# Raw slots and fixed places for the first layer's made w2 sets

## The chip, the cores and the metric

The kernel runs on one core of a Trainium2 chip. The metric is the time of one execution on the device in microseconds; the kernel before takes 1995.99 us, the median of three runs (1995.85 to 1996.73). The engines named below are PE (TensorE, matmuls), DVE (VectorE), ACT (ScalarE), POOL (GpSimd) and SP (SyncE, which here issues every DMA).

## The reference

Three layers follow one another: windowed attention, a gated layer with one expert, and a layer of eight experts whose outputs are weighted by a doubly normalised router. All data are float32.

```python
scores = scale * q @ k.T                      # 4 batches, 8 heads, 576 positions, 64 wide
mask   = (rel >= 0) & (rel < 64)              # each position sees itself and 63 before it
attn   = softmax(where(mask, scores, -1e9)) @ v
x  = attn.transpose(0, 2, 1, 3).reshape(2304, 512)

g  = x @ w_gate                               # 512 x 1536          "first layer"
x  = (g * sigmoid(g) * (x @ w_val)) @ w_out   # 1536 x 512

P  = exp(x @ r_gate - max)                    # router, 8 experts
for _ in range(8):
    P /= P.sum(1); P /= P.sum(0); P *= 2304 / 8
out = sum(P[:, e] * (relu(x @ w1[e]) @ w2[e]) for e in range(8))   # "second layer"
```

## The kernel before

**Precision.** A float32 product is made of three products of a faster type: each operand is split into a high part (a cast on ACT) and a low part (a subtraction on DVE). So every weight that is loaded is split before PE can use it.

**First layer.** The 2304 tokens are 18 tiles of 128 in five blocks (4, 4, 4, 4 and 2 tiles). A block runs 12 steps `f`, 60 steps in all; a step uses three weights: gate and value (`emit_gv`, 12 matmuls each, L788) and output (`emit_o`, 12 matmuls, L806, one step later). Each step's three places in the source are "positions", 180 in all. In block 0 the weights are read as they are, converted and stored in a DRAM buffer `saved`; in blocks 1 to 4 (from step 12) they are loaded from `saved`, 256 KB each, and split by `split_1` (ACT L605, DVE L606) two steps ahead of their use.

**Attention beside it.** Each step of the first layer carries pieces of the attention of the next block's tiles, a tile every nine positions: transposes of q and k (L297), scores (PE L320), their reduction (DVE L332, eight a tile), exponentials (ACT L409), normalisation (DVE L417, L418, L423), transposes of the result (PE L440) and the product with v (L457). After a block, the router's logits are computed from its output (L826, DVE L841, PE L853, DVE L856), and ACT copies the output from PSUM (L816) for a store to `x2d` (L818).

**The made w2 sets.** The second layer multiplies with seven combinations (a Strassen scheme) of the quarters of a pair of w2 blocks. For the experts 1 to 5 the combinations are made during the first layer and stored in the DRAM buffer `w2p`: 20 sets of two raw blocks (2 x 256 KB) that become seven pieces of 256 KB, high and low parts together. `split_w2q` (L718) makes one set in three parts: `w2_first` (ACT L678 and twice L675, DVE L687, L700, L701), `w2_second` (ACT L675, DVE twice L684) and `w2_third` (ACT twice L675, DVE L715, L716 and three times L684), and ends with one store of all seven pieces (L731, 1792 KB). It works in one of two staging places in turn (`o_stw`).

**The ring of raw slots.** All raw weights (from `saved`, the sets' two blocks, x for the second layer, the first w1 and w2) are loaded by `load_one` (L560) in the order in which they are used, each into the next slot of a ring: six slots (`o_raw`) up to step 12, then eight (`o_raw` and two of the second layer's accumulators, `o_more`) to the end of the first layer, then six again (`place_raws`). A load is issued when the use that held its slot is done; a set holds its two slots until the end of `split_w2q`.

**Order.** The source emits the pieces in the order of the positions, and a scheduler sets each engine's order from that and from what it expects to be ready; it may move an instruction ahead of others or behind them. Only where the source asks for it (`add_manual_dep` at the end) an instruction is kept behind a given one. SP's queue is in order too: a DMA that waits for its data or its slot holds up those behind it. The first layer's sets stand one after a step in two of three steps, from step 12 on, and are not tied.

Of the kernel before, what the change touches and what calls it, by code (L numbers as in the profile page):

```python
# [17 lines left out]
def attention_moe_moe2(  # L18
# [78 lines left out]
    o_ones = take("F", 128)  # L97
    o_mask = take("F", 3 * WK)
    o_logit = take("F", NTILE * NE)
    o_prob = take("F", NTILE * NE)  # L100
    o_rows = take("F", NTILE)
    o_cols = take("F", NE)
    o_part = take("F", NE)
    o_gmax = take("F", 2)
    o_stat = take("F", NSC * 3 * H)
    o_lgs = takes("F", 128, 6)
    o_wgp = take("F", KD * 32)
    NRAW = 6
# [12 lines left out]
    o_more = o_acc[4:6]  # L121
# [6 lines left out]
    o_kraw = takes("bF", 512, 3)  # L128
    o_xc = take("bR", 2 * 7 * 2 * HT)
# [18 lines left out]
    o_stw = [o_w2[0], o_w2[4]]  # L148

# [57 lines left out]
    def emit_consts():  # L207
# [19 lines left out]
        nc.gpsimd.memset(ones, 1.0)  # L227
# [292 lines left out]
    raw_at = []  # L520
    raw_prev = []
    raw_done = set()
    raw_held = set()

    def place_raws(ready):
        ring = o_raw + o_more
        last = {}
        for n in range(len(raw_keys)):
            if n < 2 * NCONV:
                o = o_raw[n % NRAW]  # L530
            elif n < ready:
                o = ring[(n - 2 * NCONV) % len(ring)]
            else:
                o = next(raw_at[i] for i in range(n - len(ring), n) if raw_at[i] in o_raw and last[raw_at[i]] == i)
            raw_at.append(o)
            raw_prev.append(last.get(o))
            last[o] = n
# [7 lines left out]
    def load_one():  # L545
        n = w_load[0]
        if n >= raw_stop[0] or n >= 2 * NCONV and raw_prev[n] is not None and raw_prev[n] not in raw_done:
            return False
        w_load[0] += 1
        key, i = raw_keys[n]  # L550
        src = sources(key)[i]
        if wide(key):
            dst = sl(o_wide[n % NWIDE], 1024).bitcast(I32)
        elif key[0] == "x":
            dst = sl(raw_at[n], HT)
        else:
            dst = sl(raw_at[n], 512)
# [50 lines left out]
    def raw_slots(key):  # L608
# [4 lines left out]
        return [raw_at[n + i] for i in range(cnt)]  # L613
# [109 lines left out]
    def split_w2q(key):  # L723
        _, e, g, j = key
        r = [sl(o, 512) for o in raw_slots(key)]
        st = o_stw[(e * NF2 // 2 + j) % 2]
        o = lambda m: st + 512 * MSEQ.index(m)
        w2_first(r, o)
        w2_second(r, o)
        w2_third(r, o)  # L730
        nc.sync.dma_start(out=kept(e, j), in_=sl(st, 7 * 512).rearrange("p (m w) -> p m w", m=7))  # L731
        load_w()
        load_w()
# [41 lines left out]
    def do_split(key):  # L775
        {"1": split_1, "w1": split_w1, "w2": split_w2, "w2q": split_w2q, "x": split_x}[key[0]](key)
# [82 lines left out]
    def emit_gmax1():  # L859
        nc.vector.tensor_reduce(sl(o_gmax, 1), logit, AX.X, ALU.max)  # L860
# [606 lines left out]
    made = [("w2q", e, 0, j) for e in range(1, NE - 2) for j in range(NF2 // 2)]  # L1467
    seq = [(b, f) for b in range(NB) for f in range(NF1)]
    prev = None
    for s, (b, f) in enumerate(seq):  # L1470
        for kind in range(3):
# [12 lines left out]
            att_at(3 * s + kind)  # L1484
        if s == 1:
# [7 lines left out]
    assert not made  # L1493
# [89 lines left out]
    raw_first = []  # L1583
    for e in ev:
# [9 lines left out]
        if e[0] == "w1n" and key is not None and not raw_first:  # L1594
            raw_first.append(len(raw_keys))
        if key is not None:
            raw_keys.extend((key, i) for i in range(len(sources(key))))

    place_raws(raw_first[0])
# [22 lines left out]
    def banks(x):  # L1622
# [46 lines left out]
        "w2h": emit_w2h,  # L1669
        "w2r": emit_w2r,  # L1670
# [14 lines left out]
    for e in ev:  # L1685
# [56 lines left out]
```

## Time and profile before

| | |
|---|---|
| time, median of three runs | 1995.99 us |
| the profiled execution | 1994.68 us |
| its span | 1992.9 us |
| busy PE, DVE, ACT, POOL | 1965.0, 1509.4, 1233.9, 41.2 us |
| DMA queue of SP | 81.2% of 16 engines' time, 527 MB |
| first layer's steps in the span | about 44 to 571 us |
| second layer | from 571 us to the end |

Times within the profile count from the span's start. A bracket `[2.85 <-DVE area_bF L423]` behind an instruction says that its engine was idle for 2.85 us before it and what ended that idle time. `area_F`, `area_aR` and so on are large tiles that the kernel cuts up itself: `area_F` holds the raw slots, `area_aR` the staging places of the sets. DRAM inputs appear without digits, so `in_moe_w_dram` stands for w1 and w2 as well.

### The profile page before, as it was taken

Reading aid. Unit: us, or ns where it says so; the run is one execution under the profiler, and the core shown is the slowest. Engines: PE = TensorE matmul, PEld = TensorE weight load, DVE = VectorE, ACT = ScalarE, POOL = GpSimd, SP = SyncE. Lnnn points to the kernel's source line nnn. Section 1 sums busy time; section 2 is a strip of 40 time slices with the busy share of each in tenths; the row PEclk is TensorE's granted clock in tenths of the full one; section 3 lists DMA queues with packets and bytes.
Section 4 is the critical chain, followed back from the end, with each engine's and each line's share of the span. In section 5 each row is a group of like instructions: output and inputs, shape, how many; then the busy total and the mean of one; then the engine's idle time right before and its main releaser. Section 6 shows DMA issues by size and latency. Waiting matters only on the chain.

```text
span 1992.9 us, 33648 instructions
## 1 busy us (share of the span) xinstructions
PE 1965.0 (99%) x11815; PEld 1855.9 (93%) x11815; DVE 1509.4 (76%) x3298; ACT 1233.9 (62%) x2795; POOL 41.2 (2%) x77
## 2 busy tenths in 40 slices
PE   8999999999999999999999999999999999999998
PEld 6887877778998999999999999999999999999998
DVE  7987777877677999989987777868777566666566
ACT  7766676766552677777764566657565455555555
POOL 3100000000000000000000000000000000000000
PEclk9999999999999999999999999999999999999999
DMA  9988889777764869979888889989877877777775
GB/s 243 280 271 253 247 230 290 240 242 222 230 225 166 302 212 296 369 244 342 264 287 268 262 301 325 333 301 333 289 248 267 279 260 261 261 260 246 268 240 170
DMA packets 303002, 529.36 MB, mean 266 GB/s; under 512 B 74976, under 2 KB 159728, under 8 KB 302320
## 3 DMA queue, kind: packets, MB, share of 16 engines
q1 hardware_dynamic: 302832, 527.21, 81.2%
q8 instruction: 93, 1.52, 0.3%
q14 instruction: 77, 0.63, 0.1%
HBM read 390.74 MB, written 136.39 MB: 265 GB/s over the span
## 4 chain that ended last, share of the span: by engine, by line
PE 91%; DVE 3%; DMA 3%; ACT 2%; issue 0%; SPq 0%; POOL 0%; DVEq 0%; ACTq 0%
PE ps L1138 34%; PE ps L1271 34%; PE ps L788 12%; PE ps L806 6%; DMA area_F<-in_moe_w_dram 2%; PE ps L965 2%; PE ps L919 2%; PE ps L457 1%; PE ps L440 1%; ACT area_bF L409 0%; PE ps L297 0%; PE ps L320 0%; PE ps L1301 0%; DVE area_R L606 0%; DVE area_bF L423 0%
## 5 line engine op out<-in xcount | busy, mean ns | idle before, releaser
L1138 PE MATMUL ps<-area_bR,area_R 128*128 128x384 f32 x3864 | 771.5, 335 | 0.0
L1271 PE MATMUL ps<-area_R 128*128 128x384 f32 x3864 | 770.6, 334 | 0.0
L1138 PEld LDWEIGHTS ps<-area_bR,area_R 128*128 128x128 f32 x3864 | 678.0, 188 | 1.6 <-ACT area_F L1306 0.3
L1271 PEld LDWEIGHTS ps<-area_R 128*128 128x128 f32 x3864 | 678.5, 188 | 0.0
L1196 DVE TENSOR_TENSOR area_R<-area_aG,area_R 128x384 fp32r<-128x384 f32 x637 | 350.9, 554 | 238.5 <-ACT area_R L1192 232.9
L1192 ACT CAST area_R<-area_aG 128x384 fp32r<-128x384 f32 x637 | 327.0, 514 | 306.3 <-PE ps L1271 256.0
L788 PE MATMUL ps<-area_R 128*128 128x512 f32 (+1 forms) x1068 | 234.8, 374 | 3.3 <-ACT area_F L793 3.3
L788 PEld LDWEIGHTS ps<-area_R 128*128 128x128 f32 x1068 | 188.2, 190 | 41.9 <-ACT area_F L793 3.9
L1261 ACT COPY area_SF<-ps 128x384 f32<-128x384 f32 x320 | 152.5, 478 | 86.8 <-PE ps L1271 84.3
L1170 DVE TENSOR_TENSOR area_aG<-area_aG 128x384 f32<-128x384 f32 x364 | 197.1, 552 | 4.3
L675 ACT CAST area_R<-area_F 128x256 fp32r<-128x256 f32 x284 | 115.4, 407 | 59.8 <-PE ps L1138 42.7
L1239 ACT COPY ps<-area_SF 128x384 f32<-128x384 f32 x280 | 135.4, 485 | 6.8 <-DVE area_SF L1265 2.6
L1148 DVE TENSOR_TENSOR area_F<-area_F,ps 128x384 f32<-128x384 f32 x184 | 101.1, 549 | 38.7 <-PE ps L1138 38.2
L684 DVE TENSOR_TENSOR area_R<-area_F,area_R 128x256 fp32r<-128x256 f32 x284 | 117.7, 416 | 12.3 <-ACT area_R L675 11.6
L806 PE MATMUL ps<-area_SR,area_R 128*128 128x512 f32 (+1 forms) x540 | 122.7, 376 | 0.2 <-ACT area_SR L797 0.2
L1150 ACT COPY area_F<-ps 128x384 f32<-128x384 f32 x184 | 88.4, 480 | 39.8 <-PE ps L1138 39.1
L1160 DVE SCALAR_TENSOR_TENSOR area_aG<-ps,area_F 128x384 f32<-128x384 f32 x182 | 100.6, 553 | 15.2 <-PE ps L1138 15.2
L806 PEld LDWEIGHTS ps<-area_SR,area_R 128*128 128x128 f32 x540 | 93.5, 190 | 18.4 <-issue 1.2
L1160 DVE SCALAR_TENSOR_TENSOR area_aG<-area_F 128x384 f32<-128x384 f32 x182 | 100.3, 551 | 1.3
L606 DVE TENSOR_TENSOR area_R<-area_F,area_R 128x512 fp32r<-128x512 f32 x108 | 74.3, 695 | 32.5 <-ACT area_R L605 20.6
L605 ACT CAST area_R<-area_F 128x512 fp32r<-128x512 f32 x108 | 65.9, 620 | 51.3 <-PE ps L788 17.6
L788 PE MATMUL ps<-area_R,area_SR 128*128 128x512 f32 (+1 forms) x372 | 81.5, 368 | 1.4 <-ACT area_R L470 1.4
(171 smaller groups left out, 1623.3 us busy)
## 6 DMA issues: line engine op xcount, KB each, us to landing
area_R<-w2p SPq DMA_DIRECT2D x322, 512.0 KB, 5.1
area_R<-w1p SPq DMA_DIRECT2D x182, 512.0 KB, 4.4
w1p<-area_R SPq DMA_DIRECT2D x98, 512.0 KB, 5.9
area_F<-in_moe_w_dram SPq DMA_DIRECT2D x160, 256.0 KB, 5.7
area_F<-saved SPq DMA_DIRECT2D x144, 256.0 KB, 4.7
w2p<-area_aR SPq DMA_DIRECT2D x20, 1792.0 KB, 9.2
w2p<-area_F SPq DMA_DIRECT2D x12, 1536.0 KB, 8.6
saved<-area_F SPq DMA_DIRECT2D x18, 512.0 KB, 6.9
```

The costliest lines, as they stand in the source:

```text
L675: nc.scalar.copy(as_r(sl(o, 256)), src)
L684: nc.vector.tensor_tensor(out=as_r(v[:, 256:512]), in0=src, in1=v[:, 0:256], op=ALU.subtract)
L788: nc.tensor.matmul(ps, lhsT=w3[:, kk, :], rhs=x3[:, kk, :], start=(i == 0), stop=(i == 3 * KD - 1))
L806: nc.tensor.matmul(PS[m][:, 0:n], lhsT=sl(o + 512 * wp + m * 128, 128, True), rhs=sl(oh + 512 * xp, n, True), start=(f == 0 and i == 0), s ...
L1138: nc.tensor.matmul(ps, lhsT=sl(o + wp * 256 + kk * 128, 128, True), rhs=sl(o_xc + xp * 14 * HT + (B_OF[m] * 2 + kk) * HT, HT, True), start ...
L1160: nc.vector.scalar_tensor_tensor(out=sl(o_c[at], HT), in0=c, scalar=0.0, in1=sl(o_p[k % 2][q_ % 2], HT), op0=ALU.max, op1=ALU.mult)
L1170: sub = lambda o, a, b: nc.vector.tensor_tensor(out=o, in0=a, in1=b, op=ALU.subtract)
L1192: nc.scalar.copy(sl(o, HT, True), src)
L1196: nc.vector.tensor_tensor(out=sl(o + HT, HT, True), in0=src, in1=sl(o, HT), op=ALU.subtract)
L1239: nc.scalar.copy(l2_bank(n, dt), macc(MSEQ[i], dt))
L1261: nc.scalar.copy(macc(m, dt), l2_bank(7 * k + i, dt))
L1271: nc.tensor.matmul(l2_bank(7 * k + i, dt), lhsT=sl(o + wp * 256 + dt * 128, 128, True), rhs=sl(jit_of[w] + hp * HT, HT, True), start=(j == ...
```

## The change

The first layer's sets leave the ring. They get raw slots of their own (two of the accumulators for the even sets; `o_spare` in another tile and `o_late` for the odd ones, where `o_late` also holds the router's small tiles later), and the ring has six slots throughout. Each set's three parts are emitted at fixed positions, two sets in nine positions; the loads of set n + 2 are emitted behind the third part of set n. The store is cut into five DMAs (two pieces after the first part, twice one after the second, one and two after the third), each emitted one part after its data. All instructions of a part on DVE, ACT and SP are kept behind the newest instruction that the source had emitted on that engine. The ones for the router's column sums are set later, in `emit_gmax1`.

```diff
-    o_ones = take("F", 128)
+    o_late = take("F", 512)
+    o_prob, o_rows, o_ones = o_late, o_late + NTILE * NE, o_late + HT
...
-    o_more = o_acc[4:6]
...
+    o_qraw2 = [o_acc[4:6], [o_spare, o_late]]
+    QSETS = [(e, j) for e in range(1, NE - 2) for j in range(NF2 // 2)]
...
-        if n >= raw_stop[0] or n >= 2 * NCONV and raw_prev[n] is not None and raw_prev[n] not in raw_done:
+        if n >= raw_stop[0] or n >= 2 * NCONV and n - NRAW not in raw_done:
...
-    def split_w2q(key):
...
-        nc.sync.dma_start(out=kept(e, j), in_=sl(st, 7 * 512).rearrange("p (m w) -> p m w", m=7))
-        load_w()
-        load_w()
+    def q_set(n):
+        e, j = QSETS[n]
+        r = [sl(o, 512) for o in o_qraw2[n % 2]]
+        return e, j, r, o_stw[n % 2], lambda m: o_stw[n % 2] + 512 * MSEQ.index(m)
+
+    def emit_qload(n):
+        if n < len(QSETS):
+            e, j, r, st, o = q_set(n)
+            for dst, src in zip(r, w2_sources(e, j)):
+                nc.sync.dma_start(out=dst, in_=src)
+
+    def emit_qstore(n, part):
+        if 0 <= n < len(QSETS):
+            e, j, r, st, o = q_set(n)
+            at = lambda i, k, d=1: sl(st + 512 * i, 512 * (k * d)).rearrange("p (k m w) -> p k m w", m=d, w=512)[:, :, 0]
+            v = kept(e, j)
+            for i, k in ((5, 2),) if part == 0 else ((0, 1), (2, 1)) if part == 1 else ((1, 1), (3, 2)):
+                nc.sync.dma_start(out=v[:, i:i + k, :], in_=at(i, k))
+
+    def emit_q(n, part):
+        e, j, r, st, o = q_set(n)
+        if part == 0:
+            emit_qstore(n - 1, 2)
+            w2_first(r, o)
+        elif part == 1:
+            emit_qstore(n, 0)
+            w2_second(r, o)
+        else:
+            emit_qstore(n, 1)
+            w2_third(r, o)
+            emit_qload(n + 2)
...
     def emit_gmax1():
+        nc.gpsimd.memset(ones, 1.0)
...
-    made = [("w2q", e, 0, j) for e in range(1, NE - 2) for j in range(NF2 // 2)]
+    sets_at = {}
+    for n in range(len(QSETS)):
+        for part, i in enumerate(((2, 3, 5), (6, 8, 9))[n % 2]):
+            sets_at.setdefault(3 * NF1 + 9 * (n // 2) + i, []).append(("q", n, part))
+    sets_at.setdefault(3 * NF1 - 3, []).append(("qload", 0))
+    sets_at.setdefault(3 * NF1, []).append(("qload", 1))
...
+            for e in sets_at.pop(3 * s + kind, []):
+                add(*e)
...
-        if s >= NF1 and s % 3 < 2 and made and (b, f) < (NB - 2, 9):
-            add("split", made.pop(0))
...
-        if e[0] == "w2h":
+        if e[0] in ("w2h", "q"):
+            engines = [mybir.EngineType.DVE, mybir.EngineType.Activation]
+            if e[0] == "q":
+                engines.append(mybir.EngineType.SP)
             for ins in added[begin:]:
-                if ins.engine in (mybir.EngineType.DVE, mybir.EngineType.Activation):
+                if ins.engine in engines:
                     tc.add_manual_dep(
```

What this makes of the queues, at three places. In the kernel after, lines are numbered a little differently: L544 is the ring's load (L560 before), L716 a set's load, L724 a set's store, L589 and L590 the split (L605, L606), L659, L662, L668 and L671 the pieces' casts and subtractions (L675, L678, L684, L687), L797, L799, L801, L802 are L793, L795, L797, L798, and L822 is the store to `x2d`.

SP's queue in the kernel before, up to the third block's end (`saved` and `in_moe_w_dram` are loads into the ring, the latter of the sets' blocks; `w2p` is the set's store):

```order
L731 DMA w2p<-area_aR 896x1x512
L560 DMA area_F<-in_moe_w_dram 128x512
L560 DMA area_F<-saved 128x512 x5
L560 DMA area_F<-in_moe_w_dram 128x512
L560 DMA area_F<-saved 128x512
L731 DMA w2p<-area_aR 896x1x512
L560 DMA area_F<-in_moe_w_dram 128x512
L560 DMA area_F<-saved 128x512
L560 DMA area_F<-in_moe_w_dram 128x512
L253 DMA area_F<-in_v_dram 128x8x64
L560 DMA area_F<-saved 128x512 x3
L818 DMA x2d<-area_F 128x4x512
```

The same stretch of SP's queue in the kernel after:

```order
L253 DMA area_F<-in_v_dram 128x8x64
L724 DMA w2p<-area_aR 128x512
L544 DMA area_F<-saved 128x512
L724 DMA w2p<-area_aR 128x512
L716 DMA area_bF<-in_moe_w_dram 128x512
L716 DMA area_F<-in_moe_w_dram 128x512
L544 DMA area_F<-saved 128x512
L724 DMA w2p<-area_aR 128x512
L724 DMA w2p<-area_aR 128x2x512
L544 DMA area_F<-saved 128x512
L724 DMA w2p<-area_aR 128x2x512
L822 DMA x2d<-area_F 128x4x512
```

Before, a set's two loads stand apart, behind the store of the set before it and among the ring's other loads; after, they stand together, the stores are small and spread, and only `saved` goes through the ring.

ACT's queue ahead of the exponentials of the tile at that block's end, before (`area_aR` is the set's staging place):

```order
L793 ACTIVATE area_F<-ps_72 128x512
L678 CAST area_aR<-area_F 128x2x256
L605 CAST area_R<-area_F 128x512
L675 CAST area_aR<-area_F 128x256 x2
L797 CAST area_SR<-area_F 128x512
L675 CAST area_aR<-area_F 128x256 x2
L409 ACT_TABLE_LOAD
L409 ACTIVATE area_bF,area_F<-area_bF,area_F 128x128 x8
```

ACT's queue at the same place, after:

```order
L662 CAST area_aR<-area_F 128x2x256
L797 ACTIVATE area_F<-ps_72 128x512
L659 CAST area_aR<-area_F 128x256
L589 CAST area_R<-area_F 128x512
L659 CAST area_aR<-area_F 128x256 x2
L801 CAST area_SR<-area_F 128x512
L409 ACT_TABLE_LOAD
L409 ACTIVATE area_bF,area_F<-area_bF,area_F 128x128 x8
```

The set's first cast moved ahead of L793, and the two casts of its third part, which stood between L797 and the exponentials, moved behind them.

DVE's queue from the last score reduction of that tile to its normalisation, before:

```order
L332 ISA area_bF,area_F<-ps_75,area_F 128x128
L332 ISA area_F 128x1
L684 TENSOR_TENSOR area_aR<-area_F,area_aR 128x256
L716 TENSOR_TENSOR area_F<-area_F 128x256
L684 TENSOR_TENSOR area_aR<-area_F,area_aR 128x256
L606 TENSOR_TENSOR area_R<-area_F,area_R 128x512
L684 TENSOR_TENSOR area_aR<-area_F,area_aR 128x256
L417 TENSOR_SCALAR area_F<-area_F 128x8
L418 RECIPROCAL area_F<-area_F 128x8
L423 TENSOR_TENSOR area_bF<-area_bF,area_F 128x1024
```

DVE's queue there after, with what stands ahead of the first reduction in the second piece:

```order
L332 ISA area_bF,area_F<-ps_75,area_F 128x128
L332 ISA area_F 128x1
L668 TENSOR_TENSOR area_aR<-area_F,area_aR 128x256
L417 TENSOR_SCALAR area_F<-area_F 128x8
L418 RECIPROCAL area_F<-area_F 128x8
L423 TENSOR_TENSOR area_bF<-area_bF,area_F 128x1024
```

```order
L799 TENSOR_TENSOR area_F<-area_F,ps_73 128x512
L590 TENSOR_TENSOR area_R<-area_F,area_R 128x512
L668 TENSOR_TENSOR area_aR<-area_F,area_aR 128x256
L802 TENSOR_TENSOR area_SR<-area_F,area_SR 128x512
L332 ISA area_bF,area_F<-ps_74,area_F 128x128
```

One piece of a set is left between the reductions and the normalisation; the third part's other instructions moved behind L423. PE's order is the same but for L853, which stands one or two matmuls earlier after three of the blocks.

## Rows read from the trace of the kernel before

**Rows 1.** Busy time in four stretches: us, each engine busy (instructions), clock, DMA share, GB/s.

```profile
44.00:160.00 116.00, 115.11 (x736) 93.55 (x737) 103.65 (x182) 80.41 (x149) 12.99 (x15) 0.97 0.91 272
160.00:505.00 345.00, 331.42 (x2035) 267.48 (x2034) 252.46 (x616) 226.38 (x517) 15.86 (x24) 1.00 0.80 246
505.00:571.00 66.00, 65.77 (x497) 62.39 (x497) 45.19 (x95) 39.96 (x84) 0.00 (x0) 1.00 0.74 240
...
660.00:1992.90 1332.90, 1327.01 (x7675) 1324.75 (x7673) 999.96 (x2155) 822.86 (x1871) 0.00 (x0) 1.00 0.82 277
```

**Rows 2.** Waits of PE from 160 to 505: us in total, times, longest.

```profile
PE ps L440 <- DVE area_bF L423: 8.4, 5, 3.5
PE ps L853 <- DVE area_F L332: 3.1, 2, 1.7
PE ps L297 <- ACT area_F L793: 1.1, 2, 0.6
PE ps L320 <- DVE area_F L841: 0.9, 1, 0.9
```

**Rows 3.** Busy time as in Rows 1, the two slices around 416.

```profile
400.00:420.00 20.00, 17.15 (x103) 13.75 (x102) 12.21 (x37) 13.05 (x35) 1.36 (x2) 0.98 0.59 183
420.00:440.00 20.00, 20.00 (x120) 15.76 (x119) 14.39 (x29) 11.54 (x23) 0.00 (x0) 0.94 0.98 323
```

**Rows 4.** PE in order of time, 402 to 422: start, duration, instructions.

```profile
406.76 1.10 PE L320 MATMUL ps<-area_F,area_bF 64*64 64x128 f32 x32
...
413.41 2.88 PE L788 MATMUL ps<-area_R,area_SR 128*128 128x512 f32 x12
419.14 1.94 PE L440 MATMUL ps<-area_F,area_bF 128*128 128x128 f32 x8 [2.85 <-DVE area_bF L423]
```

**Rows 5.** DVE in order of time, 402 to 420.

```profile
410.25 0.68 DVE L795 TENSOR_TENSOR area_F<-area_F,ps 128x512 f32<-128x512 f32 x1
...
412.27 0.68 DVE L798 TENSOR_TENSOR area_SR<-area_F,area_SR 128x512 fp32r<-128x512 f32 x1
412.87 0.28 DVE L332 CUSTOM_DVE_ANT_0 area_bF<-ps,area_F 128x128 f32<-128x128 f32 x1
```

**Rows 6.** ACT in order of time, 402 to 420.

```profile
408.52 0.62 ACT L678 CAST area_aR<-area_F 128x512 fp32r<-128x512 f32 x1 [3.71 <-DMA area_F<-in_moe_w_dram]
```

**Rows 7.** SP's issues in order of time, 395 to 420.

```profile
398.12 0.52 SPq L731 DMA_DIRECT2D w2p<-area_aR  x1
...
402.95 1.18 SPq L560 DMA_DIRECT2D area_F<-in_moe_w_dram  x1
```

**Rows 8.** Waits of ACT from 160 to 505.

```profile
ACT area_aR L678 <- DMA area_F<-in_moe_w_dram: 18.7, 11, 4.2
ACT area_aR L675 <- DMA area_F<-in_moe_w_dram: 14.8, 14, 3.8
...
ACT area_R L605 <- DMA area_F<-saved: 9.0, 5, 2.5
```

**Rows 9.** The chain of waits, 258 to 325: start, us, what.

```profile
305.79 10.20 DMA area_F<-in_moe_w_dram
```

**Rows 10.** DMA issues from 160 to 505: times, KB each, median us to landing.

```profile
w2p<-area_aR SPq DMA_DIRECT2D x19, 1792.0 KB, 9.2
area_F<-saved SPq DMA_DIRECT2D x106, 256.0 KB, 5.2
area_F<-in_moe_w_dram SPq DMA_DIRECT2D x39, 256.0 KB, 6.2
```

**Rows 11.** Waits of ACT from 505 to 571.

```profile
ACT area_R L605 <- DMA area_F<-saved: 3.5, 2, 3.1
```

**Rows 12.** DMA issues from 505 to 571.

```profile
area_F<-saved SPq DMA_DIRECT2D x25, 256.0 KB, 3.8
area_F<-in_moe_w_dram SPq DMA_DIRECT2D x16, 256.0 KB, 3.2
```

**Rows 13.** PE's groups by line and shape, 160 to 505.

```profile
L440 PE MATMUL ps<-area_F,area_bF 128*128 128x128 f32 x80 | 11.4, 289 | 8.5 <-DVE area_bF L423 8.4
```

More of the change, by code (lines that the diff above doesn't have):

```diff
@@ L96, in attention_moe_moe2 @@
     o_ident = take("F", 128)
-    o_ones = take("F", 128)
+    o_late = take("F", 512)
+    o_prob, o_rows, o_ones = o_late, o_late + NTILE * NE, o_late + HT
+    o_cols = o_rows + NTILE
+    o_part = o_cols + NE
+    o_gmax = o_part + NE
     o_mask = take("F", 3 * WK)
     o_logit = take("F", NTILE * NE)
[L100 to L104, printed above, removed]
     o_stat = take("F", NSC * 3 * H)
+    o_wgp = take("F", KD * 32 + 16)
     o_lgs = takes("F", 128, 6)
-    o_wgp = take("F", KD * 32)
     NRAW = 6
@@ L128, in attention_moe_moe2 @@
     o_kraw = takes("bF", 512, 3)
+    o_spare = take("bF", 512)
     o_xc = take("bR", 2 * 7 * 2 * HT)
@@ L226, in emit_consts @@
         nc.gpsimd.tensor_copy(sl(o_maskr + 2 * WK, WK, True), sl(o_mask + 2 * WK, WK))
-        nc.gpsimd.memset(ones, 1.0)
         nc.gpsimd.memset(sl(o_wgp, KD * 32), 0.0)
@@ L518, in attention_moe_moe2 @@
     w_next = [0]
-    raw_at = []
-    raw_prev = []
     raw_done = set()
     raw_held = set()
[L525 to L537, printed above, removed]
     def load_w():
@@ L554, in load_one @@
         elif key[0] == "x":
-            dst = sl(raw_at[n], HT)
+            dst = sl(o_raw[n % NRAW], HT)
         else:
-            dst = sl(raw_at[n], 512)
+            dst = sl(o_raw[n % NRAW], 512)
         if len(src.shape) == 3:
@@ L612, in raw_slots @@
         w_next[0] += cnt
-        return [raw_at[n + i] for i in range(cnt)]
+        return [o_raw[(n + i) % NRAW] for i in range(cnt)]
     def wr_slot(kind, b, f):
@@ L775, in do_split @@
     def do_split(key):
-        {"1": split_1, "w1": split_w1, "w2": split_w2, "w2q": split_w2q, "x": split_x}[key[0]](key)
+        {"1": split_1, "w1": split_w1, "w2": split_w2, "x": split_x}[key[0]](key)
     def emit_gv(b, f, kind):
@@ L1466, in attention_moe_moe2 @@
     }
-    made = [("w2q", e, 0, j) for e in range(1, NE - 2) for j in range(NF2 // 2)]
+    sets_at = {}
[4 more added lines that the diff above has]
+    sets_at.setdefault(3 * NF1, []).append(("qload", 1))
+    last_set = max(sets_at) + 1
+    sets_at[last_set] = [("qstore", len(QSETS) - 1, 2)]
     seq = [(b, f) for b in range(NB) for f in range(NF1)]
@@ L1488, in attention_moe_moe2 @@
             add("split", key)
-        if s >= NF1 and s % 3 < 2 and made and (b, f) < (NB - 2, 9):
-            add("split", made.pop(0))
         prev = (b, f)
-    assert not made
+    assert not sets_at
     late = [("w1", 0, 0, 2), ("w2", 0, 0, 6), ("w1", 0, 0, 3), ("w2", 0, 0, 7)]
@@ L1581, in attention_moe_moe2 @@
     assert not hooks and not att and not early and not late, (hooks, att, early, late)
-    raw_first = []
     for e in ev:
@@ L1593, in attention_moe_moe2 @@
             key = ("w2q", e[1], 0, e[2])
-        if e[0] == "w1n" and key is not None and not raw_first:
-            raw_first.append(len(raw_keys))
         if key is not None:
             raw_keys.extend((key, i) for i in range(len(sources(key))))
-    place_raws(raw_first[0])
     marked = []
@@ L1669, in attention_moe_moe2 @@
         "w2h": emit_w2h,
+        "q": emit_q,
+        "qload": emit_qload,
+        "qstore": emit_qstore,
         "w2r": emit_w2r,
```

7 lines of the change are left out of this document (removed).

## Prediction, made before the result

> **What bounds the kernel now.** I read the busy time by stage first, because an average over the whole span (TensorE 99% busy) hides where the rest is. A stage's idle time is its length less TensorE's busy time: 0.9 us from 44 to 160, 13.6 us from 160 to 505, 0.2 us from 505 to 571, and 5.9 us in the second layer, where it lies in the last output tiles [rows 1]. The diff works from step 11 of the first layer's 60, shortly before 160, to that layer's end, so at most some 14 us of waiting are within its reach. The list of TensorE's waits in that stage adds up to the same: 8.4 + 3.1 + 1.1 + 0.9 = 13.5 us, the greatest for the attention's normalised scores (L440 after L423) [rows 2]. To this comes the clock: 0.98 and 0.94 of 2.4 GHz are granted in the two slices around the wait at 416. That is some 3.2 us at the lower level, 1.2 GHz, and costs 20 x 0.02 + 20 x 0.06 = 1.6 us [rows 3].
>
> Then I followed one wait to its cause. The score matmuls L320 end at 407.86, TensorE's other work at 413.41 + 2.88 = 416.29, and L440 starts at 419.14, after 2.85 us of nothing [rows 4]. Its chain is VectorE's score reductions L332, ScalarE's exponentials L409, VectorE's L423. L332 began only at 412.87, five microseconds after its scores were there [rows 5], because ScalarE had sat 3.71 us until 408.52 on L678, the first cast of a made w2 set, waiting for that set's load [rows 6], and VectorE's share of the set stood ahead of L332 in its queue. That load was issued at 402.95, right behind the set before's 1792 KB store of 398.12 [rows 7]: a load is issued when its ring slot comes free, and the sets, which hold two slots until their last part, free them late. So it is in all the stage: ScalarE waits 18.7 + 14.8 us for w2 loads, in 25 waits [rows 8], and a load that lands in 6.2 us at the median takes up to 10.2 us there [rows 9, 10].
>
> The span is 1992.9 us and the profiled run 1994.68, so 1.8 us lie around the span and stay. The median of three runs, 1995.99, is 1.31 us above the profiled run; I take the saving off the median.
>
> **The change part by part.**
>
> *Loads of the sets.* The same 40 loads of 256 KB go into four slots of their own, each issued when set n-2 has finished its third part. Sets alternate over nine positions of the schedule, so between that point and the set's first part lie six positions or more. The 106 saved weights, three a step, take 345 us, so a position (a third of a step) is 345 / 106 = 3.25 us, and six are 19.5 us, against 6.2 us to land at the median and 10.2 at worst [rows 1, 9, 10]. The 33.5 us of ScalarE's waits go. What TensorE gets back of it: of L440's 8.4 us the two great waits, 3.5 and the 2.85 at 416, whole, and of the remaining 2.05 us in three small waits half, 1.0; the 3.1 us of L853 and the 0.9 of L320, where VectorE was late with the set's parts; the 1.1 of L297, where L793 stood behind a waiting cast [rows 2, 4]. Sum 6.35 + 1.0 + 3.1 + 0.9 + 1.1 = 12.4 us. Bounds: 0 and 13.5.
>
> *Clock.* The drop came directly after the 2.85 us wait. Without that wait I take it as gone: 1.6 us; bounds 0 and 1.6 [rows 3].
>
> *Parts at fixed places.* The instructions are the same in number and kind (six on ScalarE and ten on VectorE a set), so their busy time is no term. What they can do is stand ahead of the score chain. L332 to L440 took 419.14 - 412.87 = 6.27 us, so L332 has to start by 416.29 - 6.27 = 410.02 for no wait. In the new order VectorE has L795, one split, one 256-wide piece and L798 between the matmuls' end (406.76) and L332: four of at most the 0.68 us of L795 and L798, 2.7 us, so L332 starts near 409.5, half a microsecond in time [rows 4, 5]. Between L332 and L417 there is one piece, where there were four and a split. So no wait, but a small margin. That is why I leave half of the three small waits standing. Nothing on PE but L853 moves: it stands one or two matmuls earlier after three block ends, losing at most four matmuls of cover, 4 x 2.88/12 = 1.0 us; at least 0. I take 0.3.
>
> *Stores.* One store of 1792 KB becomes three of 256 and two of 512 KB, each issued one part after its data, so SP doesn't stand on them. Nothing waits for them but the staging slots, written again two sets later. Cost nothing, hidden by those nine positions, 29 us; the cover goes if the queue fills (a rival below).
>
> *Ring of six instead of eight.* Between 160 and 505 the ring now holds saved weights alone: six slots of 3.25 us are 19.5 us ahead, less 5.2 us to land [rows 10], no cost. In the last block it is dearer: 25 saved and 16 other loads in 66 us, 1.6 us each, so two slots less are 3.2 us less lead [rows 1, 12]. ScalarE already waits there 3.5 us in two waits, 3.1 the longest, at no cost to TensorE [rows 11, 1]. Bounds: 0, and 2 x 3.2 = 6.4 us if both grow by all of it and pass straight through. Since 3.1 us passed without a trace, I stay near the low end: 1.0.
>
> *The rest.* Moving the router's small tiles and the memset of ones on POOL costs nothing: POOL does nothing from 505 to 571, and the ones are wanted well after the router's maximum, where the memset now stands [rows 1].
>
> Sum: 12.4 + 1.6 - 0.3 - 1.0 = 12.7 us. The profiled run would be 1982.0, the median 1995.99 - 12.7 = **1983.3**. The least and the most: all waits and the clock gone at no cost, 1995.99 - 13.6 - 1.6 = 1980.8; the large terms half as large and the costs at their bounds, 6.2 + 0.8 - 1.0 - 6.4, next to nothing.
>
> **The rivals.**
>
> *Only part comes back.* The great waits go, but the margin of half a microsecond is eaten by sets that now run every period at the same point: all ten tiles of the stage (80 matmuls of L440 at eight each [rows 13]) lose 0.6 us, and the clock drops at another place. Then 12.7 - 6.0 - 0.8 = 6 us, 1990. For it: the margin. Against: five of ten tiles have no wait today though sets run beside them.
>
> *The small stores choke the queue.* The DMA engines are 0.80 busy in the stage; 0.20 x 345 us / 20 sets = 3.45 us more engine time a set would fill them, and the loads would be late however early they are issued [rows 1]. A 256 KB transfer lands in 5.2 us, the 1792 KB store in 9.2, so five small ones one after another are up to 5 x 5.2 - 9.2 = 16.8 us dearer, and at least nothing, as the bytes are the same [rows 10]. If they choke, the waits stay: 1996, no change. Against: the next stage moves the second layer's data at a higher rate, 277 GB/s against 246 [rows 1]. The Trainium skill states this rule in "DMA: Bandwidth & Descriptors", section "Measured (HBM→SBUF, 128 partitions, SWDGE, issued from GpSimd)": batch transfers to 1 MiB or more for three quarters of the peak rate. By it the old store was rightly large and the new ones are not, and the sum would be 0 instead of 12.7; the trace shows transfers overlapping, which one-at-a-time figures leave out, so I give it a small chance.
>
> *SP holds the ring (slower).* The sets' stores and loads are now tied into SP's order, 140 of them, and each waits there for ScalarE or VectorE; behind them stand the saved loads, with six slots. From the point where SP stands longer than 19.5 - 5.2 = 14.3 us on one of them, a split waits, and with it the exponentials behind it on ScalarE. If each of the ten tiles then loses what 416 lost, 2.85 us, that is 28.5 us against 14 removed: 1995.99 + 14.5 = 2010. For it: ScalarE already waits 9.0 us for saved loads here [rows 8]. Against: a part comes at most a few positions after the store's place.
>
> **How the numbers follow.** This kernel's runs tell 0.2%, 4 us, from no change: faster is under 1992.0, slower over 2000.0. Forecast 0.68, within 1980 to 1988; a part only 0.15, 1988 to 1992; choked, or balanced by new waits, 0.09 within 4 us of now, half of it just above 1992; slower 0.06; faster than 1980 0.02. Faster: 0.68 + 0.15 + 0.02 = 0.85. The range 1980 to 1992 holds 0.83.
>
> **What would show it.** Right: between about 160 and 505 TensorE's idle time falls from 13.6 to 3 us or less, ScalarE's waits for w2 loads (33.5 us) to under 5, and the granted clock is full in 400 to 440; the stage ends some 12 us earlier and everything behind keeps its length. The last block's ScalarE waits for saved weights grow from 3.5 us with TensorE's idle time under 1.5 us. Wrong: L440 still waits for L423 on most tiles (the order in the queues, not the loads, was the cause); the median time of w2 loads over 10 us (the queue); SP waiting over 14 us ahead of saved loads; or over 3 us of TensorE idle in the last block (the ring).

## The result, and the profile after

The kernel after takes 1978.48 us, the median of four runs (1977.31 to 1978.88); the kernel before took 1996.36 us in the same rounds (1995.85 to 1999.62). The ratio is 0.9907, 95% interval 0.9894 to 0.9920: 17.9 us less, where 12.7 less were forecast. The profiled execution took 1977.31 us, with a span of 1975.5, 17.3 less than before. In the kernel after, lines lie four or five further on: L792 is L788 of before, L810 is L806, L857 is L853; the splits are L589, the sets' casts L659 and L662.

Busy time by stage in the kernel after, with stages cut where its layer ends; columns as in [rows 1]:

```profile
44.00:160.00 116.00, 115.63 (x751) 94.24 (x752) 101.10 (x176) 81.47 (x156) 13.64 (x15) 1.00 0.90 279
160.00:490.00 330.00, 330.00 (x2043) 268.12 (x2042) 253.45 (x622) 226.91 (x512) 16.88 (x25) 1.00 0.80 254
490.00:553.00 63.00, 61.09 (x474) 58.06 (x473) 42.88 (x90) 37.21 (x79) 0.00 (x0) 1.00 0.73 229
```

The 13.6 us of idle TensorE between 160 and 505 are gone to the last digit, and the clock is full there. Behind the first layer everything keeps its length: 1422.7 us to the span's end, where it was 1422.2. The last block lost 1.9 us where it lost 0.2. All waits of TensorE that the kernel after has between 160 and 560 (us in total, times, longest) lie in that block:

```profile
PE ps L792 <- ACT area_F L797: 1.0, 2, 0.6
PE ps L792 <- DVE area_F L799: 0.8, 1, 0.8
```

ScalarE's waits from 160 to 490 that answer to [rows 8]; no wait for a set's load is left, where there were 33.5 us:

```profile
ACT area_R L589 <- PE ps L792: 21.8, 23, 1.5
...
ACT area_R L589 <- DMA area_F<-saved: 6.3, 4, 3.1
```

The DMA issues of the same stretch answer to [rows 10] (a quarter of the sets' loads go to another tile):

```profile
area_F<-saved SPq DMA_DIRECT2D x105, 256.0 KB, 3.4
w2p<-area_aR SPq DMA_DIRECT2D x39, 512.0 KB, 5.5
w2p<-area_aR SPq DMA_DIRECT2D x60, 256.0 KB, 3.7
area_F<-in_moe_w_dram SPq DMA_DIRECT2D x29, 256.0 KB, 3.7
```

I compared where each of the 60 steps starts in the two traces. The difference grows by 3.4 us before step 2, by 16.8 from there to step 41, where the sets end, shrinks by 1.8 in the last block, and by 1.0 more from its last step to the end of the span: 3.4 + 16.8 - 1.8 - 1.0 = 17.4.

### The profile page after: what moved, and what is told of

It is laid out like the page before. It is cut to its first block, busy times and chain, and to the rows that moved or that the text cites. A ratio compares the mean times of both kernels' runs of the same rounds, so it can differ in the third digit from the quotient of the medians.

```text
span 1975.5 us, 33856 instructions
## 1 busy us (share of the span) xinstructions
PE 1959.5 (99%) x11815; PEld 1853.0 (94%) x11815; DVE 1507.1 (76%) x3298; ACT 1234.5 (62%) x2795; POOL 46.0 (2%) x77
## 4 chain that ended last, share of the span: by engine, by line
PE 94%; DMA 2%; ACT 2%; DVE 1%; SPq 1%; issue 0%; POOL 0%; DVEq 0%; ACTq 0%
PE ps L1143 34%; PE ps L1276 34%; PE ps L792 12%; PE ps L810 7%; PE ps L970 2%; PE ps L924 2%; DMA area_F<-in_moe_w_dram 1%; PE ps L457 1%; DMA area_F<-saved 1%; PE ps L440 1%; PE ps L320 1%; PE ps L297 0%; ACT area_bF L402 0%; PE ps L1306 0%; ACT area_aF L559 0%
## 5 line engine op out<-in xcount | busy, mean ns | idle before, releaser
L792 PE MATMUL ps<-area_R 128*128 128x512 f32 (+1 forms) x1068 | 232.3, 371 | 4.6 <-ACT area_F L797 3.8
L792 PEld LDWEIGHTS ps<-area_R 128*128 128x128 f32 x1068 | 186.2, 188 | 43.1 <-ACT area_F L797 4.7
L659 ACT CAST area_R<-area_F 128x256 fp32r<-128x256 f32 x284 | 115.5, 407 | 60.4 <-PE ps L1143 40.8
L668 DVE TENSOR_TENSOR area_R<-area_F,area_R 128x256 fp32r<-128x256 f32 x284 | 118.1, 417 | 9.5 <-ACT area_R L659 8.9
L810 PE MATMUL ps<-area_SR,area_R 128*128 128x512 f32 (+1 forms) x540 | 121.8, 374 | 0.0
L810 PEld LDWEIGHTS ps<-area_SR,area_R 128*128 128x128 f32 x540 | 92.9, 189 | 17.8 <-issue 1.2
L590 DVE TENSOR_TENSOR area_R<-area_F,area_R 128x512 fp32r<-128x512 f32 x108 | 74.5, 696 | 39.1 <-ACT area_R L589 24.7
L589 ACT CAST area_R<-area_F 128x512 fp32r<-128x512 f32 x108 | 66.0, 621 | 53.6 <-PE ps L792 28.4
L792 PE MATMUL ps<-area_R,area_SR 128*128 128x512 f32 (+1 forms) x372 | 81.3, 368 | 1.9 <-ACT area_R L470 1.3
```

The lines of the kernel that those rows point to most:

```text
L659: nc.scalar.copy(as_r(sl(o, 256)), src)
L668: nc.vector.tensor_tensor(out=as_r(v[:, 256:512]), in0=src, in1=v[:, 0:256], op=ALU.subtract)
L792: nc.tensor.matmul(ps, lhsT=w3[:, kk, :], rhs=x3[:, kk, :], start=(i == 0), stop=(i == 3 * KD - 1))
L810: nc.tensor.matmul(PS[m][:, 0:n], lhsT=sl(o + 512 * wp + m * 128, 128, True), rhs=sl(oh + 512 * xp, n, True), start=(f == 0 and i == 0), s ...
```

## The experiments

Theory: the sets' loads were issued too late, and their slots and early issue cured it ("loads", later "lead"). Rivals: the fixed places, or the order that the scheduler made ("places", "order"); the small stores, because loads land sooner behind them ("stores", in the last four runs "landing"). Idle is TensorE's sum of waits from 160 to 495 (to 505 in the last four), ScalarE's waits are those for set loads with the longest of one; both are read from each run's list of waits. Each ratio is to the kernel before in the same rounds, where its median was 1993.2 to 1996.4 us; that is why times and ratios don't follow each other exactly.

| run | us | ratio, 95% | idle | ScalarE, longest |
|---|---|---|---|---|
| before | 1996.4 | 1 | 13.5 | 33.5, 4.2 |
| after | 1978.5 | 0.9907 (0.9894 to 0.9920) | 0 | 0 |
| after_again | 1976.7 | 0.9914 (0.9895 to 0.9933) | 0 | 0 |
| loads_late | 1997.6 | 1.0012 (0.9999 to 1.0025) | 14.4 | 41.8, 4.7 |
| loads_mid | 1978.7 | 0.9919 (0.9902 to 0.9936) | 0 | 0.8, 0.8 |
| untied | 1987.5 | 0.9960 (0.9946 to 0.9974) | 6.0 | 20.8, 4.1 |
| tie_sp | 1989.1 | 0.9978 (0.9966 to 0.9990) | 8.1 | 32.2, 3.4 |
| tie_compute | 1977.9 | 0.9916 (0.9903 to 0.9930) | 0 | 0 |
| one_store | 1977.5 | 0.9908 (0.9890 to 0.9926) | 0 | 0 |
| loads_only | 1978.4 | 0.9924 (0.9910 to 0.9937) | 0.2 | 11.4, 2.1 |
| ring8 | 1977.3 | 0.9910 (0.9892 to 0.9927) | 0 | 0 |
| ring8_swap | 1976.9 | 0.9915 (0.9901 to 0.9928) | 0 | 0 |
| before_small | 1978.1 | 0.9918 (0.9901 to 0.9935) | 0 | 17.1, 1.8 |
| small_same_all | 1980.6 | 0.9932 (0.9914 to 0.9950) | 0.4 | 11.6, 1.5 |
| small_same_order | 1977.7 | 0.9915 (0.9901 to 0.9930) | 0 | 7.3, 2.1 |
| swap_same_order | 1989.6 | 0.9972 (0.9961 to 0.9983) | 6.6 | 19.7, 4.3 |
| large_other_order | 2025.4 | 1.0146 (1.0127 to 1.0165) | 28.5 | 60.8, 7.6 |

**How early the loads are issued.** loads_late and loads_mid change nothing in the kernel after but the position at which a set's loads are emitted (one or three ahead of its first part instead of six); SP's tie on them stays:

```diff
-            emit_qload(n + 2)
...
+    for n in range(len(QSETS)):
+        sets_at.setdefault(3 * NF1 + 9 * (n // 2) + (1, 5)[n % 2], []).append(("qload", n))   # mid: (-1, 3)
```

> The kernel after, but each set's two loads are issued one position (some 3.2 us) ahead of its first part instead of six; slots of their own, fixed places and small stores stay. Theory 'loads': a load lands in about 6 us at the median, so ScalarE waits some 3 us for most of the 20 sets, about 40 us or more in all between 160 and 500, and TensorE is idle there again for 8 to 20 us; 1988 to 2000 us. Rival 'places': the fixed places keep the score chain ahead of a late set; ScalarE waits, TensorE is idle for under 3 us, 1978 to 1982 us.

> The kernel after, but each set's loads are issued three positions (some 9.8 us) ahead of its first part, where the kernel after has six (no wait, 1978 us) and the late version one (42 us of ScalarE waits, 1997.6 us). Theory 'lead': what counts is whether the lead covers the landing; the loads land in 3 to 6 us there, three positions do, ScalarE waits under 6 us, TensorE idle under 1.5 us between 160 and 495, 1977 to 1980 us. Rival: the gain needs all six positions, because the places themselves drift; 1984 to 1992 us.

With the loads late the whole gain is lost, though slots, places and small stores are those of the kernel after. TensorE's waits in loads_late are the two greatest of the kernel before again (L856 is L853 there):

```profile
PE ps L440 <- DVE area_bF L423: 10.1, 6, 2.7
PE ps L856 <- DVE area_F L332: 4.3, 2, 2.5
```

So places, own slots and small stores bring nothing while the loads are late. The traces say how late. Of a set's two loads, the one whose cast comes first in loads_late (L659) is issued 3.1 us before ScalarE gets there and takes 4.5 us to land (medians of the 20 sets). In loads_mid the load for L662 is issued 6.9 us ahead, with 5.0 to land: three positions are enough. In the kernel after it is 12.3 us ahead, 9.9 at least, with 4.2 to land; in the kernel before it was 4.3 ahead, with 6.0 to land.

**The ties.** untied takes all ties away, tie_sp leaves those on SP, tie_compute those on ScalarE and VectorE:

```diff
-        if e[0] in ("w2h", "q"):
+        if e[0] == "w2h":                                  # untied
...
-                engines.append(mybir.EngineType.SP)
+                engines = [mybir.EngineType.SP]            # tie_sp; tie_compute drops the line
```

> The kernel after without the ties that hold the sets' instructions at their places (ScalarE, VectorE and SP); slots of their own, early loads, small stores and the places in the source stay. Theory 'loads': with the loads early nothing on VectorE waits, wherever the scheduler puts a set; TensorE idle under 3 us between 160 and 500, 1977 to 1981 us. Rival 'places': the scheduler again puts a set's parts ahead of the score reductions, TensorE waits 5 us or more there, 1984 to 1992 us.

> The kernel after with only SP's instructions of the sets tied to their places (loads and stores), ScalarE's and VectorE's left to the scheduler. Untying all three cost about 9 us, with ScalarE waiting 20.8 us for set loads again. Theory 'loads': the ties matter through SP alone, since they are what issues the loads early; ScalarE's waits for set loads under 3 us, TensorE idle under 3 us between 160 and 495, 1977 to 1980 us. Rival 'places': the order on ScalarE and VectorE is what counts; TensorE idle 5 us or more there, 1984 to 1990 us.

> The kernel after with only ScalarE's and VectorE's instructions of the sets tied, SP's loads and stores left to the scheduler. Theory 'loads': the scheduler issues the loads late, ScalarE waits 10 us or more for them, TensorE is idle 4 us or more between 160 and 495, 1983 to 1990 us. Rival 'places': SP's order does not matter, TensorE idle under 3 us, 1977 to 1981 us.

My theory missed all three: without SP's ties alone nothing changes, and without those on ScalarE and VectorE half of the gain or more is lost. ScalarE's waits in tie_sp:

```profile
ACT area_aR L659 <- DMA area_F<-in_moe_w_dram: 12.7, 8, 3.4
ACT area_aR L659 <- DMA area_bF<-in_moe_w_dram: 11.2, 8, 3.3
ACT area_aR L662 <- DMA area_F<-in_moe_w_dram: 8.3, 9, 2.2
```

The loads are tied, and late all the same. From the issue of a set's second load to ScalarE's arrival at L662 it is 9.9 us or more in all sets of the kernel after, 2.7 to 6.9 us in tie_sp: without the ties the scheduler pulls the casts forward, towards their loads (why it puts them there isn't shown). Lead is lost from either end.

**The loads alone.** loads_only puts the sets back as they were before (whole, one behind a step, one store, ScalarE and VectorE untied), with slots of their own and loads nine positions ahead:

```diff
-            sets_at.setdefault(3 * NF1 + 9 * (n // 2) + i, []).append(("q", n, part))
+            sets_at.setdefault(3 * NF1 + 9 * (n // 2) + (2, 5)[n % 2], []).append(("q", n, part))
...
-            for i, k in ((5, 2),) if part == 0 else ((0, 1), (2, 1)) if part == 1 else ((1, 1), (3, 2)):
-                nc.sync.dma_start(out=v[:, i:i + k, :], in_=at(i, k))
+            nc.sync.dma_start(out=kept(e, j), in_=sl(st, 7 * 512).rearrange("p (m w) -> p m w", m=7))
```

> The sets as in the kernel before (whole sets, one behind a step in two of three steps, one store of 1792 KB, ScalarE and VectorE left to the scheduler), but with slots of their own and loads issued nine positions ahead, tied on SP. Theory 'loads': this alone brings most of it, ScalarE's waits for set loads under 5 us, TensorE idle under 4 us between 160 and 495, 1978 to 1982 us. Rival 'places': whole sets on VectorE still stand ahead of the score reductions at some tiles, TensorE idle 5 to 10 us there, 1984 to 1991 us.

It has the gain, though ScalarE's waits for sets, 11.4 us, are more than the theory's 5; none is over 2.1. Its DMA issues show that the loads do not land faster there, on the contrary (6.2 us in [rows 10]). They are only issued sooner, 7.2 us (median) ahead of ScalarE's arrival at L662, against 4.3 in the kernel before:

```profile
w2p<-area_aR SPq DMA_DIRECT2D x19, 1792.0 KB, 8.9
area_F<-in_moe_w_dram SPq DMA_DIRECT2D x29, 256.0 KB, 8.6
```

**The stores.** one_store is the kernel after with the large store (as in the last three lines of the diff above); before_small is the kernel before with the store cut, each piece emitted behind the part that makes it:

```diff
-        w2_first(r, o)
-        w2_second(r, o)
-        w2_third(r, o)
-        nc.sync.dma_start(out=kept(e, j), in_=sl(st, 7 * 512).rearrange("p (m w) -> p m w", m=7))
...
+        for part, store in ((w2_first, ((5, 2),)), (w2_second, ((0, 1), (2, 1))), (w2_third, ((1, 1), (3, 2)))):
+            part(r, o)
+            for i, k in store:
+                nc.sync.dma_start(out=v[:, i:i + k, :], in_=at(i, k))
```

> The kernel after with one store of 1792 KB a set, issued behind the next set's first part's place, instead of five small ones. Theory 'loads': loads issued six positions ahead (19.5 us) cover even 10 us of landing behind a large store; 1977 to 1981 us. Rival 'stores': the small stores were what let loads land in time; saved weights and set blocks land in 8 to 10 us behind the large store, ScalarE waits 15 us or more for loads, 1984 to 1996 us. By the Trainium skill's rule on batching ('DMA: Bandwidth & Descriptors', 'Measured (HBM to SBUF, 128 partitions, SWDGE, issued from GpSimd)') the large store would be the cheaper one; that would show as a lower DMA share and a time under 1977 us.

> The kernel before with its store of 1792 KB a set cut into five (two of 512 KB, three of 256 KB), each emitted behind the part that makes its data; ring, places and lead as before. Theory 'lead': the loads are still issued 2 to 10 us ahead of the cast, so ScalarE waits 15 us or more for them and TensorE 7 us or more between 160 and 505; 1988 to 1996 us. Rival 'stores': loads land in 3.7 us instead of 6.2, which is the gain; TensorE idle under 4 us there, 1978 to 1984 us.

one_store runs like the kernel after, no cheaper: 1977.5 us, with the DMA engines 0.80 busy from 160 to 490 in both. The second was the surprise: the cut brings everything, and the rival that I had dropped was right too. But the scheduler had also moved ScalarE's and VectorE's instructions in before_small. So four kernels fix the orders, by a list of the order that another kernel has:

```diff
+    for name, runs in ORDER_OF_BEFORE.items():
+        every = [ins for ins in nc.cur_bb.bb.instructions if ins.engine == getattr(mybir.EngineType, name)]
+        order = [every[i] for a, b in runs for i in range(a, b)]
+        for one, two in zip(order, order[1:]):
+            tc.add_manual_dep(two, one.name, ...)
```

small_same_all has all four queues as in the kernel before, with five stores in the place of one, one behind another; small_same_order leaves SP to the scheduler; large_other_order has the large store and the order of before_small; swap_same_order has the large store, and before's `load_w()` twice ahead of it.

> The kernel before with each set's store of 1792 KB cut into five, issued one behind another at the same place, and with TensorE, VectorE, ScalarE and SP tied to the order that they have in the kernel before. Theory 'landing': loads issued behind the cut store land earlier (4 us instead of 6), ScalarE's greatest wait for a set falls from 4 us to 2 or less, TensorE idle under 3 us between 160 and 505; 1977 to 1982 us. Theory 'order': nothing that matters has changed, TensorE idle 10 us or more, 1990 to 1996 us.

> The kernel before with the store cut into five, each behind the part that makes its data; TensorE, VectorE and ScalarE tied to the order of the kernel before, SP's order left to the scheduler. Theory 'landing': as with all queues tied, 1977 to 1982 us, TensorE idle under 3 us between 160 and 505. Theory 'order': 1988 to 1996 us.

> The kernel before with its one large store, but TensorE, VectorE and ScalarE tied to the order that they have in the kernel before with the cut store (1978.1 us). Theory 'landing': the loads land late again, ScalarE waits 25 us or more for sets, TensorE idle 7 us or more between 160 and 505; 1987 to 1996 us. Theory 'order': the moved order is the gain, 1977 to 1981 us.

> The kernel before with its large store, TensorE, VectorE and ScalarE in its order, but the two loads that follow a set emitted ahead of the set's store instead of behind it (SP's order left to the scheduler). Theory 'landing', in the form that a load suffers from standing right behind the large store: fewer late loads, TensorE idle 2 to 8 us between 160 and 505, 1980 to 1989 us. If the large store delays whatever is in flight beside it, ahead or behind: no gain, 1990 to 1996 us.

"Landing" stands: with every queue in the old order the cut takes TensorE's idle time from 13.5 to 0.4 us. The place of [rows 4 to 7] again: first, in the kernel before, the load that SP issues right behind the store of 398.12; then the same place in small_same_all, on SP and on ScalarE (L569 is L560 there, L740 the store, L687 is L678):

```profile
398.69 0.65 SPq L560 DMA_DIRECT2D area_F<-in_moe_w_dram  x1
```

```profile
382.40 4.08 SPq L740 DMA_DIRECT2D w2p<-area_aR  x5
386.53 1.56 SPq L569 DMA_DIRECT2D area_F<-in_moe_w_dram  x1
```

```profile
391.38 0.62 ACT L687 CAST area_aR<-area_F 128x512 fp32r<-128x512 f32 x1 [0.77 <-DMA area_F<-in_moe_w_dram]
```

The cast that stood 3.71 us in the kernel before stands 0.77. The load that it wants is in the kernel before the one of 398.69, not that of 402.95 which the prediction named: it lands at 408.50, 0.60 us after the store itself (407.90) and 10.38 after the store's issue, and the cast starts at 408.52. In small_same_all it lands at 391.35, 8.95 after the first piece's issue, although SP has needed 4.1 us to issue the pieces. In all eighteen traces every transfer that SP issued between 160 and 505 lands behind the one issued ahead of it, so a load behind a store lands when the store has landed, not before.

Over the 20 sets the store is done 8.3 us after its first issue, where the large one takes 9.2 (medians), and the next load lands after 9.0 us instead of 9.8. At the place above the load gains 1.4 us in this way. Another 1.5 come from a store that is issued sooner, 7.6 us ahead of the L793 before the cast (L802 there), which waits for TensorE in both traces, instead of 6.1; most likely because the set before it was less late. Together that is the 2.9 us by which the wait shrinks. Over the stage ScalarE's longest wait for a set falls from 4.2 us to 1.5. The table shows what that is worth: where no wait is over 2.1 us TensorE loses nothing or nearly so, from 3.4 us on it loses 6 us or more. In swap_same_order TensorE's idle time fell by half, as "landing" had it, with a time just above the range given for it. large_other_order, far above its range, shows the other side: the order that the scheduler makes for the small stores is much worse with the large one.

The cut doesn't make up for any lead, however short: loads_late has the small stores as well and nothing of the gain. In small_same_all the loads are issued 4.2 us ahead of ScalarE's arrival, with 4.4 to 4.7 to land (medians for either cast), where loads_late has the 3.1 and 4.5 above.

**The last block.** ring8 gives the ring two of the sets' slots once the last set is made; ring8_swap also emits a w1 block's two loads ahead of its stores:

```diff
+        ring = o_raw + (o_acc[4:6] if sets_done and n < raw_first[0] else [])
...
+        load_w()
+        load_w()
         for i, n in ((0, 1), (1, 5), (6, 1)):
             at = 512 * MU.index((j, ORDER2[i]))
             nc.sync.dma_start(out=w1p[e][:, at:at + 512 * n], in_=sl(o + 512 * i, 512 * n))
-        load_w()
-        load_w()
```

> The kernel after, but when the last set's third part is done, two of the sets' slots join the ring of raw slots until the first layer ends: eight slots in the last block, as in the kernel before. If the ring of six made the last block's 1.8 us of TensorE idle time (535 to 548): that goes, 1976 to 1977 us. If not (the loads there wait for DMA engines, or the order of ScalarE's queue makes them): the idle time stays, 1978 to 1979 us.

> The kernel after with eight slots in the last block, and the loads that follow a first-expert w1 block emitted ahead of that block's stores instead of behind them. With eight slots alone TensorE's 1.8 us of waits in the last block became one wait of 2.0 us, for a load that stood on SP behind such a store. If that store is the cause: TensorE idle under 0.5 us from 500 to the layer's end, the layer ends 1.5 to 2 us earlier, 1975.5 to 1976.8 us. If another load is late next: idle again 1 to 2 us, 1977 to 1979 us.

The chain of waits in the kernel after goes through the ring: a split on VectorE frees a slot, and the load follows at once.

```profile
529.09 0.70 DVE area_SR L590
...
529.80 3.88 DMA area_F<-saved
```

In ring8 the chain has another load, issued behind a w1 store that waited for its data, and TensorE one wait of 2.00 us in the place of three short ones:

```profile
545.27 0.02 SPq L776
545.30 0.04 issue
545.34 5.42 DMA area_F<-in_moe_w_dram
```

In ring8_swap TensorE waits for nothing between 160 and 560. Counted from step 2, its last step begins 1.9 us sooner than in the kernel after, and the layer ends 2.8 us sooner (1.1 sooner than in after_again below); in ring8 the last step begins 1.8 us sooner, but the layer ends 0.6 later. The row for ring8_swap:

```profile
490.00:553.00 63.00, 62.92 (x487) 60.27 (x486) 44.92 (x94) 39.53 (x83) 0.00 (x0) 1.00 0.75 246
```

The times can't tell these three apart; by its trace ring8_swap is the best of them, by 1.1 to 3.4 us at the layer's end. The new order with six slots wasn't run, so what the order alone would bring isn't known.

**Both kernels again**, for the start and the spread between profiles:

> The kernel before once more, for the start: in its profile the clock fell to 1.2 GHz for 6.8 us behind the 3.3 us wait near 44 us; in the kernel after, with the same wait, it did not, and in its variants it fell for 0, 3.4 or 6.8 us. If this is chance from run to run: the same wait, and one of these three lengths. If the kernel before always pays it: 6.8 us again. Without the start, the first layer's waits as in the first profile, 13 to 14 us.

> The kernel after once more, timed in the same rounds as the variants: 1977 to 1979 us, ratio 0.990 to 0.992. At the start the 3.3 us wait and a clock drop of 0, 3.4 or 6.8 us behind it; if the change had removed it, none again. The last block's idle time 1.0 to 2 us again, if it belongs to the ring of six.

before_again (1993.0 us, one execution) waited 11.6 us in the same stage, and after_again lost 0.8 us in its last block. Between these two profiles the stretch from step 2 to step 41 differs by 14.8 us, where it was 16.8 between the first two. The start is told below.

## Why the prediction was too small

**What held.** The sets' late loads were the cause, and with six positions of lead ScalarE waits for none, though the lead was never the 19.5 us that the prediction had: it is 9.9 to 16.6 us, in one set 32.2. All four groups of TensorE's waits went, and the clock is full at 400 to 440. SP doesn't hold the ring: ScalarE waits 6.3 us for saved weights, where it waited 9.0. Right in direction, wrong in size: 17.9 us against 12.7, and outside the range.

**The step that failed first is the size of the largest term, "Loads of the sets", 12.4 us.** It measured 15.1: comparing the two traces matmul by matmul, the difference grows by that much at the listed waits and at one too short for the list. Two things were wrong in it.

Half of the three small L440 waits was kept (1.0 us) for a margin of half a microsecond. In the kernel after the margin is 1.5 us: at nine of the ten tiles L423 ends 1.64 to 1.70 us before L440 starts (9.5 at the other), where it ends 0.15 before it at every tile that waited in the kernel before. So nothing was left of these waits.

And a listed wait is less than what it costs. TensorE's matmuls overlap: 80 of L440 last 289 ns each and are busy for 11.4 us, 142 ns apiece [rows 13]. The list counts from the end of the matmul ahead, which is later than the moment at which the next could have started. All ten listed waits stand behind a matmul of L788, which lasts 388 ns in the trace, while the next starts 227 ns after it where nothing waits. Measured from start to start, the ten cost 15.0 us where the list has 13.4 (13.5 with its figures rounded), 0.16 more for each. So "least and most 1980.8", the bound for all waits gone, was no bound: it took 13.6 + 1.6 off, and 15.1 + 1.7 came.

**The other terms of the stage.** The clock gave 1.7 (predicted 1.6). L853, moved earlier, cost nothing (predicted 0.3): no wait of TensorE in the kernel after stands before it. 15.1 + 1.7 is the 16.8 that was measured.

**The ring of six**, predicted 1.0, cost 1.8 in one profile and 0.8 in the other, within its bounds. The sign named for it is not clear: ScalarE's waits for saved weights in the last block, which were to grow from 3.5 us, are 2.7 in one profile and 4.2 in the other. The three waits of TensorE are gone with eight slots, so they were the ring's; as another of 2.0 us came in their place (ring8), how much of the loss the ring alone made isn't shown.

**Outside the sum.** With every term of the sum at its measured size the forecast would have been 15.1 + 1.7 - 1.8 = 15.0, or 1981.0, still within the range. What took the result out of it is a term that the prediction put at nothing: some 3.4 us of the difference between the two profiled runs lie in the start, where the queues of the two kernels differ in one memset on POOL and in nothing else, less the 1.0 at the end, which isn't settled. That makes the 17.4 of the profiles. The medians differ by 17.9; how much of the start's 3.4 is in them isn't known, since the kernel after's other three runs have a mean granted clock of 0.997 to 0.998 where the profiled one has 1.0. The stage itself differs from one execution to the next: in before_again and after_again it gave 14.8 us, 13.1 for the waits and 1.7 for a clock drop at another of them, near 292. So how near the forecast came was in part luck, either way.

**"Stores: cost nothing, hidden"** is right as a sum, since one_store runs like the kernel after, and wrong as a reading. The trace of before had the answer: the load issued half a microsecond behind the store landed half a microsecond behind it. I named the wrong load there, the one of 402.95, and so took the late issue for the cause and the store for a bystander. Either remedy is enough, earlier loads with the large store (loads_only) or the cut store with the loads where the kernel before has them, some 4 us ahead (small_same_all). So in the kernel after taking the cut away shows nothing, and taking the lead away (loads_late) shows a loss most likely because it leaves less lead than small_same_all has. The rule of the Trainium skill ("DMA: Bandwidth & Descriptors", section "Measured (HBM→SBUF, 128 partitions, SWDGE, issued from GpSimd)") on batching to 1 MiB or more, which I named beside the rival of the small stores, would have the large store be the cheaper one. Its figures are for loads issued from GpSimd. Here SP issues a store, and five pieces of 256 and 512 KB are done 0.9 us sooner than the one of 1792 KB; the measurement decides.

**"Parts at fixed places" was no term**, and right as far as the kernel after goes; but once the parts are apart, the ties on ScalarE and VectorE carry half of the gain or more (untied, tie_sp), through the distance between load and cast and not through the score chain that I weighed.

## What to carry to other kernels

When an engine waits for a load, ask two things of it: how long before its use it is issued, and what large transfer was issued just ahead of it; either may cure the wait, and an experiment that removes one cure while the other is in place can show nothing. Test a suspect on the kernel before, with the queues' orders held fixed, since the scheduler moves other instructions too when one DMA is changed. And take the price of a wait on TensorE from start to start, not from the list of idle time.

## What the runs showed of the hardware that was not expected

The wait of 3.3 us that ends near 44 us is in all eighteen profiles (3.24 to 3.31 us), and what follows it isn't the same: the granted clock stayed at 2.4 GHz in six, fell to 1.2 GHz for 3.41 us in six and for 6.83 us in six. The stretch behind it in before_again, and then in small_same_all, which has the same order in every queue up to there (columns as above, the clock is the third from the end):

```profile
44.00:52.00 8.00, 7.75 (x23) 6.11 (x24) 6.62 (x7) 4.25 (x6) 3.68 (x3) 0.63 1.11 349
```

```profile
44.00:52.00 8.00, 8.00 (x40) 6.58 (x40) 8.00 (x9) 5.56 (x9) 3.76 (x3) 1.00 1.09 360
```

Variants with the start of the kernel after show all three cases (untied, loads_mid, tie_compute), and with the order of before there is a run without a fall, so nothing in the runs ties the 3.4 us between the two profiles there to the change. What decides it stays open: both profiles of the kernel before had the long fall, both of the kernel after none.
